# Attention stage of a fused kernel: half of q's copies by DMA, output transposes in groups, epsilon on VectorE, and a new order of instructions

## The chip, the core and the metric

The kernel runs on one core of one Trainium2 chip. A core has TensorE (PE, matmuls and transposes into PSUM), VectorE (DVE), ScalarE (ACT), GpSimd (POOL) and SyncE (SP), whose queue issues all the DMAs of this kernel. Each engine works through its own queue strictly in order. The metric is the device time of one execution in microseconds, as the median of several runs.

## What is computed

```python
def _attn_ref(q, k, v):            # 2 batches, 8 heads, 1152 positions, head size 64
    q_pool = q.reshape(B, H, S // 2, 2, D).mean(axis=3)
    scores = scale * np.matmul(q_pool, k.transpose(0, 1, 3, 2))
    attn = np.exp(scores - np.max(scores, axis=-1, keepdims=True))
    attn = attn / (np.sum(attn, axis=-1, keepdims=True) + 1e-09)
    return np.matmul(attn, v)
...
x = attn_out.transpose(0, 2, 1, 3).reshape(B * S, H * D)   # 1152 x 512
h = x @ w_in;  x = (h * np.clip(h + 3, 0, 6) / 6) @ w_out  # hidden size 2048
...
# then 8 experts (512 -> 1024 -> 512) weighted by a gate that is normalised 8 times over rows and columns
```

## The kernel before

The program has three stages: attention, the two-layer network, and the experts. The change is in the first, and in the order of the second.

**Attention.** Eight pairs n of (batch, two heads) are cut into nine units each, 72 units u in all. A unit is 128 rows of scores against 1152 keys. For each unit PE computes `scores` into one of two PSUM tiles `big` (line 359, six matmuls: q and k are split into a high and a low part that together keep float32 precision), DVE takes the row extreme (`rowmax`, L369), ACT the exponential (`expo`, L378), which also adds up the row sums. Then the 128x1152 block is split into two float16 parts: `high` on ACT (L283, hl<-p), `low` mostly on POOL (L291, hl<-p,hl), and a DMA transpose turns both (`across`, L391, pt<-hl). There are four `hl` and four `pt` tiles. Some units ("T" in the table `HIGHS`) are transposed by PE instead (`flip`, L397, with `flip_high` on ACT and `flip_low` on DVE, L408). PE then multiplies by v (`pv`, L420 and L421), into one of two PSUM banks `sm`.

**The output of attention.** For each chunk c of a pair (five to a pair, the last is 64 rows) DVE adds the three parts of the product (`gather`, L442) and divides by the row sums (`norm`, L451). PE transposes the chunk (`turn`, L457) into the same `sm` bank, ACT copies its high part (`x_hi`, L467), DVE makes the low part (`x_lo`, L471), and only then is the bank free. The row sums pass through `total` on ACT (L429, adds the epsilon) and `inverse` on DVE (L432) twice to a pair.

**Preparation of the next pair.** While a pair runs, the next pair's q, k and v are loaded (L303, L298, L308). q's two positions are added (`q_sum`, L324); `q_hi` (L285 on ACT, L287 on DVE) writes q's high part for each head into two halves of the partitions, four copies to a pair; `q_lo` (L293), `k_hi` (L283), `k_lo` (L291, kt<-raw,kt), `v_r1` and `v_r2` (L291, v<-v) make the rest. The tables `PREP`, `HIGHS` and `LOWS` name the engine of each step (S is ACT, V DVE, G POOL).

**What sets the order.** Every step is an entry in a plan (`Plan.add`) with an engine, an estimated cost and its dependencies. `Plan.run` gives each a rank, the longest way to the end by those costs, and draws the steps in time order; of the steps that can start, the one of the highest rank is put next into its engine's queue. A load is planned with `LOAD`, a DMA transpose with `TURN` (lead, transfer, tail). The plan only orders: on the chip each instruction waits for semaphores.

Of the kernel before, what the change touches and what calls it, by code (L numbers as in the profile page):

```python
# [9 lines left out]
F32 = mybir.dt.float32  # L10
# [11 lines left out]
SQ = S // 2  # L22
# [3 lines left out]
TB = 384  # L26
# [5 lines left out]
NP = 3  # L32
SLOTS = {"kt": (4, 1), "v": (2, 3), "p": (NP, 1), "hl": (4, 1), "pt": (4, 1), "pf": (2, 1)}
WARM = 9
LAG, PACE, PATIENCE = 0.2, 3.2, 0.0
PV_LAG, EARLY = 4, 3
HIGHS = [
    "STSTSSSVS", "SSSSSTSSS", "SSSSSTSSS", "SVSSSSTSS", "SSSSSTSSS", "SSSSSTSSS",
    "SSSSSTSSS", "STSSSTSVS",
]  # L40
LOWS = [
    "G.G.GGGGG", "GGGGG.VGG", "GGGGG.VGG", "GGGGGV.GG", "GGGGG.VGG", "GGGGG.VGG",
    "GGGGG.VGG", "G.GGG.GVG",
]
# [14 lines left out]
class Plan:  # L59
# [58 lines left out]
    def run(self):  # L118
# [69 lines left out]
def fused_kernel(ctx, tc, qd, kd, vd, w_in, w_out, w_gate, w1, w2, out):  # L188
# [72 lines left out]
    def attention(plan, xh, xl, xs, qv, qv_used, raw_keys, extra):  # L261
# [193 lines left out]
        def turn(n, c):  # L455
            w = width(c)
            nc.tensor.transpose(  # L457
                o_t[n, c][:, 384:384 + w], x_t[n][0:w, c].rearrange("p h d -> p (h d)"), ident[0:w, 0:w]
            )

        def x_out(n, c):
# [20 lines left out]
        def load_pair(n):  # L482
            kr, qr = raw_keys(0), raw_keys(1)
            if n == 0:
                h0, h1 = rows_of
                add("SP", 0.6, load_q, n, h0, w=[(qr, 0)], dma=(0.8, 0.85, 2.5))
                add("SP", 0.6, load_k, n, h0, slice(0, TB), w=[(kr, (0, 0))], dma=(0.8, 0.3, 2.5))
                add("SP", 0.6, load_k, n, h0, slice(TB, S), w=[(kr, (0, 1)), (kr, (0, 2))], dma=(0.8, 0.6, 2.5))
                add("SP", 0.6, load_q, n, h1, w=[(qr, 1)], dma=(0.8, 0.85, 2.5))
                add("SP", 0.6, load_k, n, h1, w=[(kr, (1, i)) for i in range(3)], dma=(0.8, 0.85, 2.5))  # L490
# [11 lines left out]
        def prep(n, kr, qr):  # L502
# [5 lines left out]
            for j in (0, 1):  # L508
# [4 lines left out]
                for i in thirds:  # L513
# [4 lines left out]
                for i in (0, 1):  # L518
# [10 lines left out]
        def front(u):  # L529
            n, c, j = units[u]  # L530
            i = u % 9
            if i == 0:
                S_[n] = plan.tile("sums", 3)
            js = (0, 1) if j is None else (j,)
            ps, nb, e = plan.tile("big", 2), plan.tile("nb", 4), new_slot("p")
            q = q_key[n % 2]
            add("PE", 1.04 * len(js), scores, u, pace=("unit", PACE),
                r=[(q, ("h", jj, a)) for jj in js for a in (0, 1)] + [(q, ("l", jj)) for jj in js]
                + [K[n][jj] for jj in js] + [qv_used], w=[ps])
            add("V", 1.43, rowmax, u, r=[ps], w=[nb, e])  # L540
            add("S", 1.41, expo, u, r=[ps, nb], w=[e, (S_[n], i)])
            return e
# [792 lines left out]
```

## Time and profile before

| what | value |
|---|---|
| median of 3 runs | 1293.03 us (1292.16 to 1296.89) |
| the profiled execution, its own time | 1296.86 us |
| its span, first to last instruction | 1295.1 us |
| PE busy | 1215.5 us (94%) |
| DVE busy | 941.1 us (73%) |
| ACT busy | 499.2 us (39%) |
| POOL busy | 194.3 us (15%) |

The shares are means over three stages that differ. POOL works only in the first 310 us, which is attention. A stretch in which PE is busy throughout can be shortened only by less PE work; one in which PE has gaps can be shortened by whatever fills them. The granted clock says at which share of its full rate TensorE ran.

### The profile page before, as it was taken

The page shows a single profiled execution, that of the slowest core. Times are in us where ns is not written, and L with a number is a line of the kernel's source. Part 1 is how long each engine was busy: PE and PEld are TensorE (multiplying, and loading weights), DVE is VectorE, ACT ScalarE, POOL GpSimd, SP SyncE. Part 2 cuts the span into 40 slices and gives each one's busy share as a digit, 9 for nine tenths or more (in the row PEclk, how much of TensorE's full clock was granted, in tenths as well). Part 3 has the DMA queues.
Part 4 walks back from the last instruction along what each step waited for, and adds up shares of the span by engine and source line. Part 5 has one row for each costly group of instructions (what it writes and reads, how often), then busy time and mean ns, then how long its engine had stood idle before and what let it go on. Part 6 is the DMA issues. An engine that isn't in the chain of part 4 may idle for free.

```text
span 1295.1 us, 18865 instructions
## 1 busy us (share of the span) xinstructions
PE 1215.5 (94%) x7718; PEld 1117.1 (86%) x7718; DVE 941.1 (73%) x1529; ACT 499.2 (39%) x745; POOL 194.3 (15%) x88
## 2 busy tenths in 40 slices
PE   6878878868999999989999999999999999999998
PEld 4767777757999999988899899899889989989987
DVE  7879887768999992897685576577568558657643
ACT  6867867754432441422232233124124223223310
POOL 5856676642000000000000000000000000000000
PEclk7889988889999999899999999999999999999999
DMA  5878969878323230101111011111111102101001
GB/s 146 176 159 179 210 131 189 174 167 136 105 95 110 93 110 17 49 17 34 66 66 49 18 64 50 45 37 49 49 33 66 33 33 66 50 21 62 1 1 73
DMA packets 161589, 104.64 MB, mean 81 GB/s; under 512 B 146848, under 2 KB 146912, under 8 KB 159584
## 3 DMA queue, kind: packets, MB, share of 16 engines
q1 hardware_dynamic: 161504, 103.45, 31.8%
q8 instruction: 60, 0.98, 0.3%
q14 instruction: 25, 0.20, 0.1%
HBM read 64.50 MB, written 2.36 MB: 52 GB/s over the span
## 4 chain that ended last, share of the span: by engine, by line
PE 80%; DVE 11%; issue 4%; DMA 3%; ACT 2%; POOL 1%; SPq 0%; DVEq 0%; POOLq 0%; ACTq 0%
PE sm L1164 30%; PE prod L1081 26%; PE big L816 8%; PE big L613 8%; PE sm L420 3%; DVE p L369 3%; PE big L359 2%; PE sm L421 2%; DMA pt<-hl 2%; DMA v<-vd 1%; DVE v L291 1%; ACT p L378 1%; PE sm L1196 1%; ACT hl L283 1%; DVE sm L442 1%
## 5 line engine op out<-in xcount | busy, mean ns | idle before, releaser
L1164 PE MATMUL sm<-w2h,slot 128*128 128x512 f32 x1152 | 355.0, 389 | 0.0
L1164 PEld LDWEIGHTS sm<-w2h,slot 128*128 128x128 f32 x1152 | 216.3, 188 | 44.6
L1164 PE MATMUL sm<-w2l,slot 128*128 128x512 f32 x576 | 224.2, 389 | 0.0
L1171 DVE SCALAR_TENSOR_TENSOR slot<-sm,gate,slot 128x512 f32<-128x512 f32 x120 | 89.9, 749 | 175.1 <-PE sm L1164 175.1
L1081 PE MATMUL prod<-xh,w_all 128*128 128x288 f32 x1024 | 194.7, 299 | 0.8 <-DVE slot L1100 0.6
L1081 PE MATMUL prod<-slot,w_all 128*128 128x288 f32 x1152 | 161.8, 293 | 0.0
L1081 PEld LDWEIGHTS prod<-xh,w_all 128*128 128x128 f32 x1024 | 158.8, 192 | 2.3 <-PE sm L1243 1.2
L1051 ACT CAST w2h<-raw 128x512 fp32r<-128x512 f32 x64 | 39.8, 623 | 303.3 <-PE sm L1164 296.9
L1081 PEld LDWEIGHTS prod<-slot,w_all 128*128 128x128 f32 x1152 | 155.1, 188 | 0.1
L291 POOL TENSOR_TENSOR hl<-p,hl 128x1152 f16<-128x1152 f32 x55 | 137.0, 2497 | 94.5 <-ACT hl L283 83.2
L359 PE MATMUL big<-kt,ql 128*128 128x384 f32 x240 | 97.9, 408 | 34.8 <-ACT p L378 26.6
L1164 PEld LDWEIGHTS sm<-w2l,slot 128*128 128x128 f32 x576 | 108.2, 188 | 21.9
L1100 DVE TENSOR_TENSOR slot<-slot,prod 128x576 f32<-128x576 f32 x160 | 119.6, 749 | 9.2 <-PE prod L1081 6.5
L420 PE MATMUL sm<-v,pt 128*128 128x192 bf16 (+1 forms) x630 | 101.0, 255 | 14.0 <-DVE pf L408 6.7
L1081 PE MATMUL prod<-xl,w_all 128*128 128x288 f32 x512 | 111.2, 299 | 0.0
L369 DVE TENSOR_SCALAR_CACHE_REDUCE p<-big 128x1152 bf16<-128x1152 f32 x72 | 96.8, 1350 | 15.8 <-PE big L359 11.5
L378 ACT ACTIVATE p<-big,nb 128x1152 f32<-128x1152 f32 x72 | 87.9, 1221 | 34.9 <-DVE p L369 34.7
L613 PE MATMUL big<-xh,w_all 128*128 128x384 f32 x384 | 100.3, 338 | 1.1 <-DVE slot L603 0.5
L421 PE MATMUL sm<-v,pt 128*128 128x128 bf16 (+1 forms) x630 | 98.8, 224 | 0.0
L359 PEld LDWEIGHTS big<-kt,ql 128*128 128x128 f32 x240 | 51.7, 215 | 45.2 <-ACT p L378 34.0
L359 PE MATMUL big<-kt,qh 128*128 128x384 f32 x240 | 89.8, 374 | 0.0
L1081 PEld LDWEIGHTS prod<-xl,w_all 128*128 128x128 f32 x512 | 83.9, 191 | 0.0
(124 smaller groups left out, 1860.4 us busy)
## 6 DMA issues: line engine op xcount, KB each, us to landing
raw<-w SPq DMA_DIRECT2D x64, 512.0 KB, 3.7
raw<-w_out SPq DMA_DIRECT2D x8, 1024.0 KB, 4.7
raw<-w_in SPq DMA_DIRECT2D x7, 1024.0 KB, 4.9
v<-vd SPq DMA_DIRECT2D x8, 576.0 KB, 4.7
raw<-qd SPq DMA_DIRECT2D x7, 576.0 KB, 4.6
raw<-kd SPq DMA_DIRECT2D x7, 576.0 KB, 4.7
out<-slot SPq DMA_DIRECT2D x8, 256.0 KB, 2.0
raw<-w_in SPq DMA_DIRECT2D x2, 512.0 KB, 5.3
```

The lines of the kernel that those rows point to most:

```text
L291: engines[eng].tensor_tensor(out, a, b, op=ALU.subtract)
L359: nc.tensor.matmul(ps[:, s, :TB], lhs, rhs[:, s * TB:(s + 1) * TB], start=m == 0, stop=m == len(mms) - 1,)
L369: nc.vector.tensor_scalar(waste, ps[:, :, :TB], PSHIFT * math.log(2.0), None, op0=ALU.add, op1=ALU.min, accum_out=nb)
L378: nc.scalar.activation(e_t[u], ps_t.pop(u)[:, :, :TB], AF.Exp, bias=nb_t.pop(u), scale=-1.0, accum_out=sums[n][:, i:i + 1])
L420: nc.tensor.matmul(ps, tt[:, k, q], vs, start=k == 0, stop=False)
L421: nc.tensor.matmul(ps[:, 0:2 * D], tt[:, NKC + k, q], vs[:, 0:2], start=False, stop=k == NKC - 1)
L613: nc.tensor.matmul(ps[t], lhs[:, ks], rhs[:, k, t * TB:(t + 1) * TB], start=k == 0 and m == 0, stop=k == KD - 1 and m == 2,)
L816: nc.tensor.matmul(downs[x, c][:, t, :TB], lhs[:, cs], rhs[:, t * TB:(t + 1) * TB], start=f == first and m == 0, stop=f == last and m == 2,)
L1081: nc.tensor.matmul(bank(q, p)[:, h], lhs, rhs[:, k, 288 * h:288 * h + 288], start=k == 0 and m == 0, stop=k == 1 and m == 2,)
L1100: nc.vector.tensor_tensor(base()[to], base()[u], bank(q, p), op=op)
L1164: nc.tensor.matmul(ps, lhs[:, ts], rhs, start=f == 0 and m == 0, stop=f == 3 and m == 2)
L1171: nc.vector.scalar_tensor_tensor(a, ps, gt, a, op0=ALU.mult, op1=ALU.add)
```

## The change

Five things change, all in attention. Two of the four copies of q's high part (from the second pair on) are no longer made by ACT or DVE but copied across partitions by a DMA on SP's queue (`q_dup`, "D" in `PREP`). The `turn` of four chunks goes into one `sm` bank of its own, so a pair has two turns, two `x_hi` and two `x_lo` in place of five of each (the last pair has three). `total` is gone from ACT: `inverse` adds the epsilon on DVE ahead of the reciprocal. The tables of engines are new: `v_r1` goes from POOL to DVE for seven pairs, one `k_lo` of each of these pairs from POOL to DVE, `q_sum` for five pairs from DVE to POOL; 12 units in place of 10 are transposed by PE. And the plan has a longer tail for loads, other costs for `scores` and `pv`, and a table `BIAS` that is added to the ranks by the name of a step.

```diff
-LAG, PACE, PATIENCE = 0.2, 3.2, 0.0
+LAG, PACE, PATIENCE = 0.2, 3.4, 0.0
+LOAD, TURN = (0.8, 1.7, 5.5), (0.8, 3.2, 0.8)
...
-    "STSTSSSVS", "SSSSSTSSS", "SSSSSTSSS", "SVSSSSTSS", "SSSSSTSSS", "SSSSSTSSS",
+    "STSTSVSSS", "TSSSSTSSS", "STSSSSSSS", "STSSSTSSS", "STSSSTSSS", "STSSSSSSS",
...
-    "SSVVVSSSSVVGG", "SSGGVSVSSVVGV", "SSGGVVSSSVVGV", "SSGGVSVSSVVGV", "SSVGVSSSSVVGV", "SSGGVVSVSVVGV",
+    "SSVVVSSVSVVGG", "VSGVGVDDVVVVV", "SSGVGSDDSVVVV", "VSGVVSDDSVVVV", "SSVVGSDDSVVVV", "SSGVGSDDVVVVV",
...
+BIAS = {
+    "rowmax": -1.2, "pv": 10.0, "q_sum": 5.8, "inverse": -9.4, "turn": 7.5,
...
+TURNS = [((0, 1, 2, 3), (4,)), ((0, 1), (2, 3), (4,))]
...
+        for o in ops:
+            rank[o["i"]] += BIAS.get(o["fn"].__name__, 0.0)
...
+        def q_dup(n, j, i):
+            q = qh[n % 2]
+            nc.sync.dma_start(out=f32(q[rows_of[i], j, cols_of[j]]), in_=f32(q[rows_of[j], j, cols_of[j]]))
...
-        def total(n, cols):
-            nc.scalar.activation(sums[n][:, cols], sums[n][:, cols], AF.Identity, bias=eps, scale=1.0)
-
         def inverse(n, cols):
+            nc.vector.tensor_scalar_add(sums[n][:, cols], sums[n][:, cols], EPS * 2.0 ** PSHIFT)
             nc.vector.reciprocal(sums[n][:, cols], sums[n][:, cols])
...
+        def turn(n, cs):
+            t = r_t[n, cs[0]] = small()
+            for i, c in enumerate(cs):
+                w = width(c)
+                nc.tensor.transpose(t[:, 128 * i:128 * i + w], x_t[n][0:w, c].rearrange("p h d -> p (h d)"), ident[0:w, 0:w])
...
+                    if e[f"q{j}{i}"] == "D":
+                        add("SP", 0.6, q_dup, n, j, i, r=[(q, ("h", j, j)), qv_used], w=[(q, ("h", j, i))], dma=(0.8, 0.5, LOAD[2] - 0.5))
+                        continue
...
-            add("PE", 1.04 * len(js), scores, u, pace=("unit", PACE),
+            add("PE", 1.12 * len(js), scores, u, pace=("unit", PACE),
...
+            for cs in TURNS[n == np_ - 1]:
+                if c == cs[-1]:
+                    out = plan.tile("sm", 2)
+                    parts = [(p, 5 * b + i) for i in cs]
+                    add("PE", 0.12 * len(cs), turn, n, cs, r=[(x, i) for i in cs] + [qv_used], w=[out])
+                    add("S", 0.13 + 0.13 * len(cs), x_hi, n, cs, r=[out], w=[(xs, ("h",) + i) for i in parts])
```

What this does to the queues is seen at three places. SP's queue before, from the load of the second pair's k on (`v<-vd` is the load of v, `raw<-kd` and `raw<-qd` of k and q, `pt<-hl` a transpose):

```order
L298 DMA raw<-kd 128x1152
L391 DMA_TRANSPOSE pt<-hl 128x18x128 x4
L298 DMA raw<-kd 128x1152
L303 DMA raw<-qd 128x1152
L391 DMA_TRANSPOSE pt<-hl 128x18x128 x8
L308 DMA v<-vd 128x1152
L298 DMA raw<-kd 128x1152
L303 DMA raw<-qd 128x1152
L391 DMA_TRANSPOSE pt<-hl 128x18x128 x7
```

SP's queue with the change, from the first transpose on (L410 is the transpose, L346 the copy `q_dup`, L323 the load of v, L313 of k, L318 of q):

```order
L410 DMA_TRANSPOSE pt<-hl 128x18x128 x2
L346 DMA qh_95<-qh_95 64x576 x2
L313 DMA raw<-kd 128x1152
L410 DMA_TRANSPOSE pt<-hl 128x18x128 x3
L318 DMA raw<-qd 128x1152
L410 DMA_TRANSPOSE pt<-hl 128x18x128 x2
L313 DMA raw<-kd 128x1152
L410 DMA_TRANSPOSE pt<-hl 128x18x128
L346 DMA qh_94<-qh_94 64x576
L410 DMA_TRANSPOSE pt<-hl 128x18x128
L346 DMA qh_94<-qh_94 64x576
L410 DMA_TRANSPOSE pt<-hl 128x18x128
```

The load of the fourth pair's k (the third `raw<-kd` before, the second here) goes from behind twelve transposes to behind seven; the load of the third pair's v, the next row of the queue, goes from behind twelve to behind ten, and the copies of q stand between transposes.

DVE's queue before, from the row extreme of unit 18 to that of unit 20 (L442 is `gather`, L451 `norm`, `v<-v` here is `v_r2`):

```order
L369 TENSOR_SCALAR p,nb<-big 128x1152
L293 SCALAR_TENSOR_TENSOR ql_98<-raw,qh_96 64x576
L408 TENSOR_TENSOR pf<-sm,pf 128x384
L432 RECIPROCAL sums<-sums 128x4
L442 TENSOR_REDUCE sm<-sm 128x128
L451 TENSOR_TENSOR x<-sm,sums 128x128
L369 TENSOR_SCALAR p,nb<-big 128x1152
L432 RECIPROCAL sums<-sums 128x5
L434 COPY sums<-sums 64x1
L291 TENSOR_TENSOR v<-v 128x1152
L369 TENSOR_SCALAR p,nb<-big 128x1152
L471 TENSOR_TENSOR xl<-sm,xh 128x128
```

DVE's queue with the change, from the row extreme of unit 18 to that of unit 20 (L388 is `rowmax`, L448 adds the epsilon, `v<-v` here is `v_r1`, `kt<-raw,kt` a `k_lo`):

```order
L388 TENSOR_SCALAR p,nb<-big 128x1152
L459 TENSOR_REDUCE sm<-sm 128x128
L468 TENSOR_TENSOR x<-sm,sums 128x128
L448 TENSOR_SCALAR sums<-sums 128x5
L449 RECIPROCAL sums<-sums 128x5
L451 COPY sums<-sums 64x1
L306 TENSOR_TENSOR v<-v 128x1152
L388 TENSOR_SCALAR p,nb<-big 128x1152
L459 TENSOR_REDUCE sm<-sm 128x128
L468 TENSOR_TENSOR x<-sm,sums 128x128
L339 TENSOR_TENSOR raw<-raw 128x576
L388 TENSOR_SCALAR p,nb<-big 128x1152
```

The epsilon is now a DVE row ahead of the reciprocal, no `xl<-sm,xh` stands here any more, and the `v<-v` in front of a row extreme is one that reads the load itself and not POOL's result.

ACT's queue before, over units 18 to 21 (`ACTIVATE p,sums` is `expo`):

```order
L378 ACTIVATE p,sums<-big,nb 128x1152
L283 CAST hl<-p 128x1152
L429 ACTIVATE sums<-sums,eps 128x5
L283 CAST kt<-raw 64x1152
L378 ACTIVATE p,sums<-big,nb 128x1152
L283 CAST kt<-raw 64x1152
L467 CAST xh<-sm 128x128
L283 CAST hl<-p 128x1152
L378 ACTIVATE p,sums<-big,nb 128x1152
L285 ACTIVATE qh_97<-raw 64x576
L283 CAST hl<-p 128x1152
L378 ACTIVATE p,sums<-big,nb 128x1152
```

ACT's queue with the change, over units 18 to 23 (L397 is `expo`, L298 a `high` or `k_hi`, L424 `flip_high`):

```order
L397 ACTIVATE p,sums<-big,nb 128x1152
L298 CAST hl<-p 128x1152
L298 CAST kt<-raw 64x1152
L397 ACTIVATE p,sums<-big,nb 128x1152
L300 ACTIVATE qh_95<-raw 64x576 x2
L397 ACTIVATE p,sums<-big,nb 128x1152
L424 CAST pf<-sm 128x384 x2
L298 CAST hl<-p 128x1152
L424 CAST pf<-sm 128x384
L397 ACTIVATE p,sums<-big,nb 128x1152
L298 CAST hl<-p 128x1152
L397 ACTIVATE p,sums<-big,nb 128x1152
```

Between two exponentials ACT now mostly holds one `high`; the epsilon is gone and `xh<-sm` is met twice to a pair.

## Rows read from the trace of the kernel before

**Rows 1.** Stretches: start:end, length, busy PE, PEld, DVE, ACT, POOL, clock, DMA, GB/s.

```profile
0.00:16.00 16.00, 8.14 (x20) 5.58 (x21) 11.58 (x16) 6.67 (x11) 6.83 (x13) 0.79 0.63 185
16.00:301.00 285.00, 226.30 (x1846) 202.49 (x1846) 225.76 (x345) 205.24 (x312) 184.77 (x74) 0.89 0.83 168
301.00:331.00 30.00, 24.77 (x244) 22.70 (x245) 27.79 (x57) 11.81 (x23) 2.70 (x1) 1.00 0.76 153
331.00:1295.00 964.00, 956.34 (x5612) 886.33 (x5609) 675.97 (x1114) 275.49 (x399) 0.00 (x0) 0.99 0.15 51
```

**Rows 2.** Waits in 16 to 301 us: engine, line, waited for, us, times, longest.

```profile
PE big L359 <- ACT p L378: 26.6, 18, 5.0
...
PE sm L457 <- DVE x L451: 9.0, 7, 2.3
POOL v L291 <- DMA v<-vd: 8.1, 1, 8.1
PE sm L420 <- DVE xl L471: 8.0, 5, 2.0
...
DVE sums L432 <- ACT sums L429: 7.2, 3, 2.7
...
ACT kt L283 <- DMA raw<-kd: 3.4, 2, 2.7
PE sm L397 <- DVE xl L471: 3.2, 2, 2.8
```

**Rows 3.** Timeline 79 to 92 us, SP, POOL, ACT, DVE: start, length, instruction, idle before.

```profile
80.09 0.57 SPq L308 DMA_DIRECT2D v<-vd  x1
...
84.78 2.11 POOL L291 TENSOR_TENSOR v<-v 128x1152 f32<-128x1152 f32 x1 [8.13 <-DMA v<-vd]
...
86.11 1.15 ACT L283 CAST kt<-raw 64x1152 fp32r<-64x1152 f32 x1 [2.74 <-DMA raw<-kd]
...
79.78 1.36 DVE L369 TENSOR_SCALAR_CACHE_REDUCE p<-big 128x1152 bf16<-128x1152 f32 x1 [0.30 <-PE big L359]
...
86.92 3.67 DVE L291 TENSOR_TENSOR v<-v 128x1152 bf16<-128x1152 f32 x1 [3.15 <-POOL v L291]
90.48 1.35 DVE L369 TENSOR_SCALAR_CACHE_REDUCE p<-big 128x1152 bf16<-128x1152 f32 x1
```

**Rows 4.** Groups by form, 16 to 301 us: count, busy us, mean ns, idle before.

```profile
L397 PE MATMUL sm<-ident,p 128*128 128x128 f32 x81 | 12.8, 288 | 6.2 <-DVE xl L471 3.2 <-DVE pf L408 2.7
L285 ACT ACTIVATE qh<-raw 64x576 fp32r<-64x576 f32 x23 | 15.7, 681 | 4.6 <-DVE raw L324 4.3
L291 DVE TENSOR_TENSOR v<-v 128x1152 bf16<-128x1152 f32 x7 | 17.5, 2506 | 3.2 <-POOL v L291 3.1
L291 DVE TENSOR_TENSOR hl<-p,hl 128x1152 f16<-128x1152 f32 x6 | 10.3, 1722 | 1.2 <-ACT hl L283 0.7 <-DMA raw<-qd 0.5
L291 DVE TENSOR_TENSOR kt<-raw,kt 64x1152 fp32r<-64x1152 f32 x1 | 1.4, 1351 | 0.0
L324 DVE TENSOR_TENSOR raw<-raw 128x576 f32<-128x576 f32 x7 | 13.8, 1974 | 0.1
L408 DVE TENSOR_TENSOR pf<-sm,pf 128x384 f16<-128x384 f32 x27 | 14.4, 549 | 0.6 <-ACT pf L405 0.5
L432 DVE RECIPROCAL sums<-sums 128x5 f32<-128x5 f32 x7 | 1.3, 186 | 7.2 <-ACT sums L429 7.2
L471 DVE TENSOR_TENSOR xl<-sm,xh 128x128 fp32r<-128x128 f32 x27 | 7.5, 285 | 9.6 <-ACT xh L467 9.5
L471 DVE TENSOR_TENSOR xl<-sm,xh 128x64 fp32r<-128x64 f32 x6 | 1.3, 218 | 1.4 <-ACT xh L467 1.4
```

**Rows 5.** Line 291 up to 320 us: shortest/median/longest ns.

```profile
L291 POOL TENSOR_TENSOR hl<-p,hl x55: 2361/2383/4257, 19.6 to 310.0; 128x1152 f16<-128x1152 f32 x55
...
L291 DVE TENSOR_TENSOR v<-v x7: 1476/2098/3673, 31.5 to 268.4; 128x1152 bf16<-128x1152 f32 x7
```

**Rows 6.** DMA issues up to 330 us: count, KB each, median us to landing.

```profile
raw<-qd SPq DMA_DIRECT2D x2, 288.0 KB, 4.4
```

More of the change, by code (lines that the diff above doesn't have):

```diff
@@ L53 @@
 }
+BIAS = {
+    "rowmax": -1.2, "pv": 10.0, "q_sum": 5.8, "inverse": -9.4, "turn": 7.5,
+    "gate_l": -7.6, "q_dup": 12.1, "v_r1": -7.6, "dec_low": 3.9, "dec_rest": 7.0,
+    "total": 11.6, "norm": 8.7, "load_k": -0.8, "load_q": 8.4, "flip": -8.8,
+    "k_lo": 9.9, "dec_scale": 3.8, "dec_m": -1.9, "x_lo": -0.2, "low": 8.9,
+    "x_hi": 8.4, "gather": -4.5, "up_one": -1.6, "dec_e": -0.8, "load_v": -3.4,
+    "expo": -8.5, "across": 7.3, "gate_m": -0.4, "dec_high": -0.7, "flip_high": 12.8,
+    "dec_sign": 13.6, "k_hi": 12.8, "gate_s": -6.1, "gate_h": 8.4, "v_r2": 2.2,
+    "q_lo": -2.5, "dec_join": 14.2, "q_hi": 8.9, "scores": 7.4, "flip_low": 1.0,
+    "high": 3.5,
+}
+TURNS = [((0, 1, 2, 3), (4,)), ((0, 1), (2, 3), (4,))]
 W2_TILES = 6
@@ L211, in fused_kernel @@
     nc.vector.memset(half, 0.5)
-    eps = per.tile([128, 1], F32, name="eps")
-    nc.vector.memset(eps, EPS * 2.0 ** PSHIFT)
     rebias = per.tile([128, 1], F32, name="rebias")
@@ L343, in attention @@
             units.append((n, 4, None))
-        ps_t, nb_t, sums, e_t, h_t, p_t, o_t, x_t, f_t = {}, {}, {}, {}, {}, {}, {}, {}, {}
+        ps_t, nb_t, sums, e_t, h_t, p_t, o_t, x_t, f_t, r_t = {}, {}, {}, {}, {}, {}, {}, {}, {}, {}
         def scores(u):
@@ L453, in norm, with x_out, x_hi, x_lo @@
             )
[L455 to L461, printed above, removed]
+        def turn(n, cs):
[3 more added lines that the diff above has]
+                nc.tensor.transpose(t[:, 128 * i:128 * i + w], x_t[n][0:w, c].rearrange("p h d -> p (h d)"), ident[0:w, 0:w])
+        def x_out(n, cs):
             b, p = pairs[n]
-            return o_t[n, c][:, 384:384 + width(c)], (p, slice(b * SQ + 128 * c, b * SQ + 128 * c + width(c)))
-        def x_hi(n, c):
-            ps, (p, o) = x_out(n, c)
+            w = 64 if cs[0] == 4 else 128 * len(cs)
+            return r_t[n, cs[0]][:, 0:w], (p, slice(b * SQ + 128 * cs[0], b * SQ + 128 * cs[0] + w))
+        def x_hi(n, cs):
+            ps, (p, o) = x_out(n, cs)
             nc.scalar.copy(xh[:, p, o], ps)
-        def x_lo(n, c):
-            ps, (p, o) = x_out(n, c)
+        def x_lo(n, cs):
+            ps, (p, o) = x_out(n, cs)
             nc.vector.tensor_tensor(xl[:, p, o], ps, f32(xh[:, p, o]), op=ALU.subtract)
@@ L485, in load_pair @@
                 h0, h1 = rows_of
[L486 to L490, printed above, removed]
+                add("SP", 0.6, load_q, n, h0, w=[(qr, 0)], dma=(0.8, 0.85, LOAD[2]))
+                add("SP", 0.6, load_k, n, h0, slice(0, TB), w=[(kr, (0, 0))], dma=(0.8, 0.3, LOAD[2]))
+                add("SP", 0.6, load_k, n, h0, slice(TB, S), w=[(kr, (0, 1)), (kr, (0, 2))], dma=(0.8, 0.6, LOAD[2]))
+                add("SP", 0.6, load_q, n, h1, w=[(qr, 1)], dma=(0.8, 0.85, LOAD[2]))
+                add("SP", 0.6, load_k, n, h1, w=[(kr, (1, i)) for i in range(3)], dma=(0.8, 0.85, LOAD[2]))
             else:
@@ L517, in prep @@
                             w=[(t, ("h", p)) for p in ps], share=share)
-                for i in (0, 1):
+                for i in (j, 1 - j):
+                    if e[f"q{j}{i}"] == "D":
+                        add("SP", 0.6, q_dup, n, j, i, r=[(q, ("h", j, j)), qv_used], w=[(q, ("h", j, i))], dma=(0.8, 0.5, LOAD[2] - 0.5))
+                        continue
                     prep_op("q_hi", e[f"q{j}{i}"], q_hi, n, j, e[f"q{j}{i}"], i, r=[(qr, j), qv_used], w=[(q, ("h", j, i))])
@@ L566, in rear @@
             for u in us:
-                add("PE", 2.6 / len(us), pv, u, r=[P[u], V[n]], w=[(sm, "a")])
+                add("PE", 2.8 / len(us), pv, u, r=[P[u], V[n]], w=[(sm, "a")])
             if c in (0, 2):
@@ L570, in rear @@
                 parts = [(s, i) for i in range(cols.start, cols.stop)]
-                add("S", 0.2, total, n, cols, w=parts)
-                add("V", 0.17, inverse, n, cols, w=parts + ([(s, 9)] if c == 2 else []))
+                add("V", 0.25, inverse, n, cols, w=parts + ([(s, 9)] if c == 2 else []))
             add("V", 0.565, gather, n, c, r=[(sm, "a")], w=[(sm, "b")])
             add("V", 0.29, norm, n, c, r=[(sm, "b"), qv_used] + [(s, i) for i in ((2 * c, 2 * c + 1) if c < 4 else (8, 9))], w=[(x, c)])
-            add("PE", 0.15, turn, n, c, r=[(x, c), qv_used], w=[(sm, "b")])
             b, p = pairs[n]
-            part = (p, 5 * b + c)
-            add("S", 0.26, x_hi, n, c, r=[(sm, "b")], w=[(xs, ("h",) + part)])
-            add("V", 0.285, x_lo, n, c, r=[(sm, "b"), (xs, ("h",) + part)], w=[(xs, ("l",) + part)])
+            for cs in TURNS[n == np_ - 1]:
[4 more added lines that the diff above has]
+                    add("S", 0.13 + 0.13 * len(cs), x_hi, n, cs, r=[out], w=[(xs, ("h",) + i) for i in parts])
+                    add("V", 0.13 + 0.14 * len(cs), x_lo, n, cs, r=[out] + [(xs, ("h",) + i) for i in parts],
+                        w=[(xs, ("l",) + i) for i in parts])
         pending = []
```

8 lines of the change are left out of this document (4 added, 4 removed).

## The prediction

> **What bounds the kernel now.** I read the stretches first [rows 1]. From 331 us to the end PE is busy for 956 of 964 us at a clock of 0.99, so nothing that the change moves there can win more than 8 us, and I count that part as unchanged. Attention's steady part, 16 to 301 us, is another matter: DVE, the busiest, has 225.8 us of work in 285, PE 226.3, ACT 205.2, POOL 184.8. No engine is full. The time is made by engines that wait for each other in order, and PE's 58.7 us without work, at a clock of 0.89, are all that can be won there. The 72 units take 4.0 us each.
>
> The second view is who waits for whom in that stretch [rows 2]. PE waits 26.6 us for an exponential that frees its score tile. PE also waits where the output leaves: 9.0 us for `norm` before a `turn`, and 8.0 and 3.2 us for `x_lo` to free an `sm` bank. DVE waits 7.2 us, in three waits, for the epsilon on ACT. POOL stands 8.1 us in one wait for a load of v.
>
> The third view is the timeline of the widest gap between two row extremes, 79.78 to 90.48 us [rows 3]. The load of v is issued at 80.09 behind the transposes, POOL's `v_r1` can start at 84.78 only, DVE's `v_r2` stands in its queue behind that until 86.92 and takes 3.67 us, and the next row extreme comes at 90.48. On ACT a k load that is 2.74 us late holds the next exponential.
>
> **The change part by part.** The epsilon: `total` leaves ACT, so the three waits of DVE go: **-7.2 us** [rows 2]. What takes their place is an add in DVE's own queue, counted below.
>
> The turns: 40 round trips PE, ACT, DVE, PE become 17 (two for each of seven pairs, three for the last), and a bank of `pv` is free after `norm` and not after `x_lo`. Of the 20.2 us that PE waits in these three rows [rows 2] I take off the share of trips that go, 23 of 40: **-11.6 us**. The bounds are 0, if the same stall moves to the new bank, of which there are still two for all uses, and 20.2.
>
> The late landings: loads of k stand earlier in SP's queue and `v_r1` is planned for a later landing. The gap of 10.7 us [rows 3] against 4.0 for a unit gives **-6.7 us**; 0 if another wait ends last there, 10.1 with ACT's 3.4 us for k [rows 2] on top.
>
> ACT's work: 15 of the 27 `q_hi` go from ACT, at 0.681 us [rows 4] 10.2 us of its 205, 5%. I take 5% off PE's 26.6 us of waiting for the exponential: **-1.3 us**. At best half of that wait goes, 13.3.
>
> DVE's work, what speaks against: seven `v_r1` come from POOL, at the 2.506 us of `v_r2`, which has the same shape in: 17.5. Seven `k_lo` come too; DVE ran one of that form, in 1.351, and the same operation on 128 partitions (`low`) in 1.722 on the mean; I take 1.722, since the one had a lucky place: 12.1. Four `low` go (-6.9) and five `q_sum` at 1.974 (-9.9). Six more `flip_low` at 0.549 are 3.3, sixteen adds of the epsilon at most a reciprocal's 0.186 each, 3.0. `x_lo` costs 0.285 for 128 columns and 0.218 for 64, so about 0.69 for 512 and 0.42 for 256: -3.5 over all pairs. One `q_hi` and two `k_hi` more, under `k_lo`'s 1.351 each, 3.0 together. The sum is 18.6 [rows 4]. Part of it falls into DVE's idle time; I put on the path DVE's busy share, 225.8 of 285 or 0.79: **+14.7 us**. The bounds are 0 (all of it into the 59 us that DVE idles) and 24.1 (`k_lo` at 2.506 too, all on the path).
>
> Why such an operation takes 1.476 us at its shortest and 2.506 on the mean: POOL runs 2.383 us pieces beside it [rows 4, 5]. The Trainium skill says on "SBUF — State Buffer", section "SBUF: two separate sides", that VectorE operations with two SBUF inputs and GpSimd's share one port pair as an exclusive lock that is held for the whole instruction. The trace agrees in direction, with 1.0 us lost on the mean and not a whole piece of POOL. By the rule at its worst the sum would end slower; that is the first rival.
>
> What I count at nothing: the 14 copies of q by DMA. The nearest load, 288 KB, lands in 4.4 us [rows 6]; the third pair's copies stand behind the eighth and ninth transposes, and its own first transpose is the fifteenth, so five to six units of 4.0 us lie between. Without that cover each of seven pairs would start up to 4.4 us late, 31 us. Each issue takes SP some 0.57 us [rows 3], 8 in all, spread over 285. Six more PE transposes of three blocks for two units more are 18 at 0.288 us, 5.2 at most [rows 4], hidden in PE's 58.7 us without work; if PE were full they would cost that. The last pair sends nine blocks by DMA transpose and not seven, and DVE is busy there for 27.8 of 30 us [rows 1]; PE's 5.2 us without work there are what can be won, and I take the like for a loss: 0, plus or minus 5. A better clock would come with shorter gaps: 0.10 of PE's 226 us, up to 23, but only where PE is what ends last; 0.
>
> **The sum.** -7.2 - 11.6 - 6.7 - 1.3 + 14.7 = -12.1 us, against the profiled execution's own 1296.9: 1284.8. That execution lies 3.8 above the median of 1293.0, so the forecast is 1281. All gains at their best and DVE's work hidden would be -51 (7.2 + 20.2 + 10.1 + 13.3), 1242; only the epsilon's gain and 24.1 on the path +17, 1310.
>
> **The rivals.** First, slower: DVE becomes the bound because what came from POOL waits behind POOL. If each of the 14 operations waits for a whole piece, `v_r1` takes 1.476 + 2.383 and `k_lo` 1.351 + 2.383 us: 53.1 in place of 29.6, DVE's addition 42.1 and not 18.6. At 0.79 of that on the path against the 26.8 of gains it gives +6.5, 1299; with all of it +15.3, 1308; I call it 1304. For it: the longest of them took 3.673 [rows 5], and they stand right in front of a row extreme. Against it: POOL loses 14 operations, so there is less to wait behind. It decides from an addition of 34 us on (26.8 / 0.79). This is the lock as the Trainium skill states it on "SBUF — State Buffer", taken at its worst.
>
> Second, no change: the stalls move and do not go. DVE's work of 225.8 + 18.6 = 244.4 us needs an idle share under 12% to make the stretch shorter by more than 7 us (244.4 / 0.88 = 278), and above 16% the stretch is longer (291). Today it is 21%. Between these two it gives 1287 to 1299, about 1293. For it: ACT and DVE still serve one score tile of two in turn. Against it: the waits of the first three terms have a cause that is taken away.
>
> Third, a larger gain: with shorter round trips PE gets the whole 20.2 us and half the 26.6 back, the added DVE work falls half into idle time (9.3): -7.2 - 20.2 - 6.7 - 13.3 + 9.3 = -38, 1255; halfway to the forecast, 1268, is what I expect of it. For it: gaps feed on each other in queues, and PE runs at 0.89. Against it: at 1268 DVE would have to be busy for 94% of the stretch (244.4 of 260).
>
> The copies of q may land late after all: up to +31 less 12, 1312. Their place in the queue speaks against it.
>
> **How the numbers follow.** The forecast's case, 1272 to 1287, 0.45; the larger gain 0.17; no change 0.20; DVE behind POOL 0.15; late copies 0.03. A measurement of this kernel tells about 0.5% (6.5 us) from no change; the three runs lie 0.4% apart. Faster by more than that is 0.45 + 0.17 = 0.62, within it 0.20, slower 0.18. The range leaves out the outer half of the two slower cases and the tail of the larger gain: 1259 to 1303; the forecast's own is 1272 to 1287.
>
> **What would show it.** In the profile after: no wait of DVE's reciprocal for ACT; PE's waits for `norm` and `x_lo` together under 10 us; no wait of several us on a load of v or k; 17 `x_lo`; DVE's busy time up to 331 us some 19 us higher, or more if `v_r1` and `k_lo` on DVE average above 2.5 us, which is the first rival; no wait of PE on a copy of q. The start of the stretch in which PE is never idle, 331 us now, should come about 12 us earlier. The forecast is wrong if DVE's waiting for PE and for ACT's high copies grows by what the terms take away.

## The result, and the profile after

| | before | with the change |
|---|---|---|
| median | 1293.9 us (4 runs, 1292.2 to 1296.9) | 1277.6 us (4 runs, 1275.0 to 1279.8) |
| ratio | | 0.986, 95% interval 0.984 to 0.989 |

The change makes the kernel 1.4% faster, 16.3 us, where 12 were forecast. The stretches of the changed kernel, cut where those of [rows 1] were cut (columns as there):

```profile
0.00:16.00 16.00, 7.22 (x16) 4.95 (x17) 11.99 (x16) 5.98 (x10) 6.68 (x13) 1.00 0.55 152
16.00:285.00 269.00, 223.92 (x1871) 201.17 (x1871) 244.28 (x358) 192.95 (x271) 168.34 (x66) 0.93 0.93 181
285.00:315.00 30.00, 26.49 (x246) 24.59 (x244) 24.05 (x47) 9.13 (x15) 4.71 (x2) 0.96 0.71 144
315.00:1277.00 962.00, 954.24 (x5608) 882.73 (x5606) 676.80 (x1116) 275.92 (x399) 0.00 (x0) 1.00 0.15 52
```

The last stretch, in which PE is never idle, is as long as before (962 against 964 us) and begins 16 us earlier. So the whole gain lies in attention's steady part, 269 us against 285. PE's work in it is the same (223.9 against 226.3 us, at a granted clock of 0.93 against 0.89); DVE has 18.5 us more work and idles for 9% instead of 21%.

The waits of that part (engine, line, waited for, us, times, longest), which answer to [rows 2]:

```profile
ACT p L397 <- DVE p L388: 56.6, 34, 5.7
...
PE big L378 <- ACT p L397: 21.9, 17, 3.1
...
PE sm L416 <- DVE x L468: 4.8, 4, 2.0
...
PE sm L476 <- DVE x L468: 2.9, 2, 1.5
ACT hl L298 <- DMA pt<-hl: 2.7, 3, 1.7
...
PE sm L439 <- DVE xl L489: 1.3, 1, 1.3
...
PE sm L416 <- DVE xl L489: 0.2, 1, 0.2
```

L476 is `turn`, L439 `pv`, L416 `flip`. The waits that the forecast named are smaller or gone: no reciprocal waits for ACT, none on a load of v or k stands here any more, and the waits for `norm` and `x_lo`, 20.2 us before, are 2.9, 1.3 and 0.2, with 4.8 new where a `flip` waits for `norm` to free a bank. One wait that it did not name fell too, that of ACT's `high` for a DMA transpose to free an `hl` tile. It is 2.7 us here. And one wait grew, that of ACT's exponential for DVE's row extreme, as fits a stretch in which DVE has become the busiest engine. The rows of before:

```profile
ACT p L378 <- DVE p L369: 31.6, 29, 6.1
...
ACT hl L283 <- DMA pt<-hl: 20.8, 8, 6.3
```

DVE's groups by form (columns as [rows 4]), again from 16 to 285 us of the changed kernel:

```profile
L306 DVE TENSOR_TENSOR kt<-raw,kt 64x1152 fp32r<-64x1152 f32 x8 | 18.4, 2300 | 0.2
L306 DVE TENSOR_TENSOR v<-v 128x1152 bf16<-128x1152 f32 x7 | 12.8, 1828 | 0.0
L306 DVE TENSOR_TENSOR v<-v 128x1152 f32<-128x1152 f32 x7 | 11.2, 1594 | 0.1
...
L448 DVE TENSOR_SCALAR sums<-sums 128x5 f32<-128x5 f32 x7 | 6.7, 957 | 0.0
L448 DVE TENSOR_SCALAR sums<-sums 128x4 f32<-128x4 f32 x8 | 5.9, 740 | 0.0
L489 DVE TENSOR_TENSOR xl<-sm,xh 128x512 fp32r<-128x512 f32 x7 | 4.8, 680 | 0.0
```

The two rows of L448 are the surprise: an add over four or five columns takes 0.74 and 0.96 us on the mean, 12.6 us together. Over the whole of attention, up to 331 us before and up to 315 with the change, DVE's busy time rises by 15.2 us, 265.1 to 280.3, where 18.6 were forecast. Of q's new copies little is to be seen: a copy of 144 KB lands 2.8 us after its issue, and nothing waits for one.

The gap of 10.7 us in [rows 3], which the prediction calls the widest, is the second widest of before: the starts of the row extremes show nine gaps of over 6 us there, and the widest, 11.9, begins at 274.9 us. With the change there are seven, the widest 9.0.

One sentence on the change ahead of the prediction is wrong, and the prediction drew on it: the plan has no longer tail for loads. The new table `LOAD` with 5.5 us stands at the head of the file, but a line `LOAD = (0.8, 1.7, 2.5)` further down, which the diff does not touch and so does not show, hides it in the function that makes the plan. The late landings are not counted at all.

### The profile page after: what moved, and what is told of

It is laid out like the page before. It is cut to its first block, busy times and chain, and to the rows that moved or that the text cites. A ratio compares the mean times of both kernels' runs of the same rounds, so it can differ in the third digit from the quotient of the medians.

```text
span 1277.9 us, 18850 instructions
## 1 busy us (share of the span) xinstructions
PE 1211.9 (95%) x7736; PEld 1113.4 (87%) x7736; DVE 957.1 (75%) x1534; ACT 484.0 (38%) x694; POOL 179.7 (14%) x81
## 4 chain that ended last, share of the span: by engine, by line
PE 75%; DVE 16%; issue 4%; DMA 2%; ACT 1%; POOL 1%; SPq 0%; POOLq 0%; DVEq 0%; ACTq 0%
PE sm L1188 31%; PE prod L1105 26%; PE big L840 7%; PE big L637 4%; DVE p L388 4%; PE big L378 3%; PE sm L439 2%; DMA pt<-hl 2%; DVE kt L306 1%; PE sm L440 1%; DVE sm L459 1%; DVE sums L448 1%; DVE pf L427 1%; DVE v L306 1%; DVE slot L630 1%
## 5 line engine op out<-in xcount | busy, mean ns | idle before, releaser
L1188 PE MATMUL sm<-w2h,slot 128*128 128x512 f32 x1152 | 355.0, 389 | 0.0
L306 POOL TENSOR_TENSOR hl<-p,hl 128x1152 f16<-128x1152 f32 x57 | 146.9, 2585 | 102.5 <-ACT hl L298 76.0
L1188 PEld LDWEIGHTS sm<-w2l,slot 128*128 128x128 f32 x576 | 108.1, 188 | 21.9
L378 PE MATMUL big<-kt,ql 128*128 128x384 f32 x240 | 96.0, 400 | 27.2 <-ACT p L397 21.9
L397 ACT ACTIVATE p<-big,nb 128x1152 f32<-128x1152 f32 x72 | 87.9, 1221 | 60.0 <-DVE p L388 59.4
L388 DVE TENSOR_SCALAR_CACHE_REDUCE p<-big 128x1152 bf16<-128x1152 f32 x72 | 96.9, 1350 | 16.8 <-PE big L378 14.8
L439 PE MATMUL sm<-v,pt 128*128 128x192 bf16 (+1 forms) x612 | 98.5, 257 | 8.2 <-DVE pf L427 4.7
```

Of the source, the lines that this page charges most:

```text
L306: engines[eng].tensor_tensor(out, a, b, op=ALU.subtract)
L378: nc.tensor.matmul(ps[:, s, :TB], lhs, rhs[:, s * TB:(s + 1) * TB], start=m == 0, stop=m == len(mms) - 1,)
L388: nc.vector.tensor_scalar(waste, ps[:, :, :TB], PSHIFT * math.log(2.0), None, op0=ALU.add, op1=ALU.min, accum_out=nb)
L397: nc.scalar.activation(e_t[u], ps_t.pop(u)[:, :, :TB], AF.Exp, bias=nb_t.pop(u), scale=-1.0, accum_out=sums[n][:, i:i + 1])
L439: nc.tensor.matmul(ps, tt[:, k, q], vs, start=k == 0, stop=False)
L1188: nc.tensor.matmul(ps, lhs[:, ts], rhs, start=f == 0 and m == 0, stop=f == 3 and m == 2)
```

## The experiments

Every kernel is an edit of the changed one; ratios are to the kernel before, measured again beside each (medians 1294.2 to 1295.9 us), with their 95% intervals. The last column is the start of the last row extreme, from the `rowmax` line of each profile; the last instruction of the profiled execution comes 989 to 996 us after it, but for one kernel (e2, 1006), so it says where the time went. A profile is of one execution; the changed kernel's took 1279.7 us, 2.1 above its median.

| run | edit | median us | ratio | last row extreme, us |
|---|---|---|---|---|
| (before) | | 1293.9 | 1 | 306.1 |
| (changed) | | 1277.6 | 0.986 (0.984 to 0.989) | 287.5 |
| e6_no_bias | `BIAS` empty | 1301.2 | 1.004 (1.002 to 1.005) | 309.3 |
| e11_bias_nine_tenths | `BIAS` times 0.9 | 1286.0 | 0.993 (0.991 to 0.995) | 292.6 |
| e10_late_counted | the local `LOAD` taken out | 1279.8 | 0.990 (0.987 to 0.994) | 286.1 |
| e4_turns_single | one turn for each chunk | 1314.8 | 1.015 (1.013 to 1.018) | 313.5 |
| e12_no_bias_turns_single | both e6 and e4 | 1315.8 | 1.016 (1.013 to 1.019) | 317.6 |
| e1_eps_on_act | the add on ACT | 1277.5 | 0.987 (0.985 to 0.989) | 285.4 |
| e3_no_eps | no add | 1263.1 | 0.975 (0.974 to 0.977) | 269.4 |
| e2_eps_accumulating | add in its accumulating form, new tile | 1280.3 | 0.988 (0.987 to 0.990) | 273.1 |
| e5_eps_accumulating_in_place | the same without a new tile | 1268.4 | 0.979 (0.976 to 0.981) | 273.3 |
| e7_v_r1_on_pool | `v_r1` on POOL | 1272.3 | 0.983 (0.980 to 0.986) | 278.6 |
| e9_best | e5 and e7 | 1271.5 | 0.982 (0.980 to 0.984) | 273.4 |
| e8_q_copies_on_act | q's copies on ACT | 1278.1 | 0.987 (0.984 to 0.989) | 281.9 |

The theory to be tested was that of the prediction: the time comes from stalls that the parts of the change remove, less DVE's added work. The main rival was that the gain comes from the order, whatever the parts do.

**The order.** In e6 all parts stay and the table is empty:

```diff
-BIAS = {
-    "rowmax": -1.2, "pv": 10.0, "q_sum": 5.8, "inverse": -9.4, "turn": 7.5,
...
+BIAS = {}
```

> The changed kernel with the table of biases empty, so the plan orders by its costs alone; all parts of the change are in. If the parts make the gain, as the prediction's terms have it, 1278 to 1284. If the drawn order makes it, this run loses most of the gain: 1290 or more.

Waits of e6 from 16 to 307 us (L368 is `scores`, L288 `high`, L438 the add):

```profile
PE big L368 <- ACT p L387: 28.8, 17, 6.4
ACT hl L288 <- DMA pt<-hl: 22.1, 10, 4.1
...
DVE sums L438 <- ACT p L387: 6.8, 5, 3.9
```

Without the table the parts are 0.4% slower than the kernel before, and the waits for the exponential and for the `hl` tiles are back at 28.8 and 22.1 us; the adds now wait 6.8 us for an exponential's row sums. All of the gain, 23.6 us against e6, is there only with the table. Whether it states rules or fits one drawing was asked with e11, which multiplies each value by 0.9:

```diff
-            rank[o["i"]] += BIAS.get(o["fn"].__name__, 0.0)
+            rank[o["i"]] += 0.9 * BIAS.get(o["fn"].__name__, 0.0)
```

> The changed kernel with every value of BIAS times 0.9, a control for what a new drawing of the order costs by itself. If the table states a rule about which step goes first, nine tenths of it say nearly the same: 1274 to 1283. If the table fits one drawn order, it gives much of the gain back: 1285 to 1300, between the changed kernel and the one without the table (1301), with PE waiting for the exponential for over 25 us.

Waits of e11 from 16 to 290 us:

```profile
PE big L378 <- ACT p L397: 14.3, 12, 4.4
PE sm L416 <- DVE pf L427: 10.0, 6, 3.3
PE sm L416 <- DVE x L468: 9.8, 5, 2.9
PE sm L476 <- DVE x L468: 7.5, 6, 1.9
...
PE sm L439 <- DMA qh<-qh: 7.0, 1, 7.0
```

1286.0: a tenth off its values loses half of the 16 us that the changed kernel gains, as expected of a table that fits one drawing. The rival said that PE would wait over 25 us for the exponential; it waits 14.3, so that part of it is wrong. Other waits took over, one of them on a late copy of q by DMA, 7.0 us. From this control on, a difference of up to some 8 us between two kernels that draw different orders says little about the edit between them.

The third drawing is e10, in which the late landings are counted after all:

```diff
-    LOAD = (0.8, 1.7, 2.5)
+    pass
```

> The changed kernel without the local line LOAD = (0.8, 1.7, 2.5), which hides the table of the same name at the head of the file, so that the plan now does count 5.5 us behind a load; the order is drawn anew, nothing else. Theory of the prediction's third term (counting late landings takes the gaps at k and v away): the waits for loads in the changed kernel's steady stretch are already small (POOL 7.0 us once, ACT 0.5), so at most 2 to 7 us, 1271 to 1276. Rival (the table BIAS fits the one order that it was drawn with, and any other order loses what it gave): between 1285 and 1301, with more gaps over 6 us than the 7 of the changed kernel and no wait on a load behind them.

Waits of e10 from 16 to 284 us:

```profile
PE big L378 <- ACT p L397: 24.5, 15, 3.8
ACT hl L298 <- DMA pt<-hl: 16.0, 13, 4.9
```

1279.8, between both expectations and not told apart from the changed kernel: the intervals overlap. Counting the landings wins nothing here, and it does not lose as much as the rival said either: it has seven gaps of over 6 us, as many as the changed kernel. So the table is not tied to one drawing alone; this other drawing keeps most of the gain, while e11's loses half of it. ACT's wait for `hl` tiles is at 16.0 us again, and the time hardly moved, so that wait alone does not explain the table's gain. Which of the waits does stays open.

**The turns.** e4 goes back to one turn for each chunk, in its own order:

```diff
-TURNS = [((0, 1, 2, 3), (4,)), ((0, 1), (2, 3), (4,))]
+TURNS = [((0,), (1,), (2,), (3,), (4,))] * 2
```

> The changed kernel with one chunk to a turn again, each in an sm bank of its own (five turns, five x_hi and five x_lo to a pair); the plan draws a new order for it with the same biases. By the prediction's term the round trips cost 11.6 us, less what DVE already has them at: 1277.6 + 11.6 + 2.8 (3.5 us of x_lo at 0.79) = 1292. The rival, that the new order made the gain and the grouping none, gives 1278 to 1281.

Waits of e4 from 16 to 315 us:

```profile
ACT hl L298 <- DMA pt<-hl: 18.7, 8, 5.4
PE sm L476 <- DVE x L468: 18.0, 10, 4.3
DVE sm L459 <- PE sm L440: 17.9, 14, 3.3
```

The stall at the turn is back, 18.0 us where 2.9 were. But 37 us is far above the forecast's 20.2 at most, and the order was drawn anew with a table made for other steps. e12 takes the table out of the comparison with both edits:

> The changed kernel with BIAS empty and with a turn for each chunk, to be read against the run with BIAS empty alone (1301.2). The prediction's second term (23 of 40 round trips, 11.6 us, up to 20.2): 1313, up to 1321, with PE waiting for norm and x_lo for about 20 us. Rival (what single turns cost with the table, 37 us, was mostly the new order): within 5 us of 1301.

Waits of e12 from 16 to 315 us (L466 is `turn`, L479 `x_lo`):

```profile
ACT hl L288 <- DMA pt<-hl: 35.3, 15, 5.7
...
PE sm L466 <- DVE x L458: 13.8, 8, 2.8
...
PE sm L406 <- DVE xl L479: 7.4, 5, 2.7
```

1315.8 against e6's 1301.2: grouping the turns is worth 14.6 us without the table, inside the forecast's bounds and near its 11.6, and PE's waits for `norm` and `x_lo` are 21.2 us again. This pair too differs in its drawing, so the 14.6 carry the control's uncertainty. The rest of e4's 37 us is the table, which does not fit single turns: with it they take as long (1314.8) as without it.

**The epsilon.** e1 puts only the add back on ACT, at its place in the order:

```diff
-            nc.vector.tensor_scalar_add(sums[n][:, cols], sums[n][:, cols], EPS * 2.0 ** PSHIFT)
+            nc.scalar.activation(sums[n][:, cols], sums[n][:, cols], AF.Identity, bias=eps, scale=1.0)
```

> The changed kernel with the epsilon added on ACT again, at the place in the order where DVE adds it; all else stands where it stood. By the prediction's term DVE waits for ACT again (7.2 us before the change) and sheds the adds, which it put at 3.0 us: about 1277.6 + 5 = 1283. The rival is that the adds on DVE cost what the wait cost: the changed kernel's trace shows 12.8 us for 16 of them (149 ns the shortest, 2396 ns the longest), so shedding them gives back more than the wait takes: 1270 to 1278.

The wait of the reciprocal (L451) for ACT in e1:

```profile
DVE sums L451 <- ACT sums L450: 9.9, 12, 1.6
```

The wait is back, and the time is the same: 1277.5. So this edit is worth nothing as made, since DVE pays as much for the adds as it waited. Why an add of five columns can cost so much is seen in the timeline of the changed kernel, at three of the sixteen (start, length, instruction; the rows of POOL and of L448 alone):

```profile
49.49 2.37 POOL L306 TENSOR_TENSOR hl<-p,hl 128x1152 f16<-128x1152 f32 x1 [1.25 <-ACT hl L298]
50.97 0.92 DVE L448 TENSOR_SCALAR sums<-sums 128x5 f32<-128x5 f32 x1
...
163.81 2.38 POOL L306 TENSOR_TENSOR hl<-p,hl 128x1152 f16<-128x1152 f32 x1 [2.06 <-ACT hl L298]
166.96 0.16 DVE L448 TENSOR_SCALAR sums<-sums 128x4 f32<-128x4 f32 x1
...
261.54 4.85 POOL L306 TENSOR_TENSOR hl<-p,hl 128x1152 f16<-128x1152 f32 x2 [4.43 <-DVE x L468]
264.03 2.39 DVE L448 TENSOR_SCALAR sums<-sums 128x5 f32<-128x5 f32 x1
```

The first add starts in the middle of a POOL piece and ends with it, at 51.89 against 51.86. The second starts when POOL is between two pieces and takes 0.16. The third ends with POOL's second piece, 266.42 against 266.39. Seven of the sixteen are held up so, each until 0.03 us after a piece has ended; nine take 0.15 to 0.20 us. The add waits for the whole rest of POOL's piece.

The Trainium skill says on "SBUF — State Buffer", section "Who interferes with whom", that VectorE's `tensor_scalar`, but not the form that also writes out its accumulator, can take the port pair that it shares with GpSimd, and that whichever of the two comes first then holds it for its whole instruction while the other is blocked. The trace agrees with the blocking, in these seven adds. e3, e2 and e5 test the rest of it. e3 leaves the epsilon out of the row sums:

```diff
-            nc.vector.tensor_scalar_add(sums[n][:, cols], sums[n][:, cols], EPS * 2.0 ** PSHIFT)
```

> The changed kernel with the addition of the epsilon left out (the row sums go into the reciprocal as they are), all else in place. The same 12.8 us of DVE go entirely: 1266 if DVE's busy share sets the time, 1278 if the wait only moves to the next instruction of DVE that needs what POOL holds (then v_r1, v_r2, k_lo and q_lo on DVE get longer by about as much).

1263.1, 14.5 us faster than the changed kernel, for 12.8 us of adds. e2 keeps the add and gives it an accumulator that nobody reads:

```diff
-            nc.vector.tensor_scalar_add(sums[n][:, cols], sums[n][:, cols], EPS * 2.0 ** PSHIFT)
+            junk = ap.tile([128, 1], F32, tag="junk", name="junk", bufs=2)
+            nc.vector.tensor_scalar(
+                sums[n][:, cols], sums[n][:, cols], EPS * 2.0 ** PSHIFT, None, op0=ALU.add, op1=ALU.min, accum_out=junk
+            )
```

> The changed kernel with the epsilon added on DVE in the form that also writes an accumulator (as the row extreme does), result the same. If the 12.8 us of the 16 adds are a wait for POOL that depends on the form of the instruction, they fall to about 0.17 us plus 0.08 us for the accumulator, 4 us in all, and with DVE busy for 91% of the stretch the time falls by some 8 us, to 1270. If any small operation at that place waits so, the adds stay at some 12 us and the time at 1278. If DVE's share is not what ends last, the adds get short and the time stays at 1278.

The last row extreme comes 14 us earlier than in the changed kernel, but the median is 1280.3. The gain is lost much later, in the experts. Their largest group of matmuls in the changed kernel, and then in e2:

```profile
L1188 PE MATMUL sm<-w2h,slot 128*128 128x512 f32 x1152 | 355.0, 389 | 0.0
```

```profile
L1191 PE MATMUL sm<-w2h,slot 128*128 128x512 f32 x1152 | 363.0, 397 | 0.0
```

The same 1152 matmuls take 397 ns each and not 389, at the same granted clock of 1.00. The only thing that e2 adds beside the adds' form is the tile `junk`, two buffers of 4 bytes a partition; e1, e3 and e4, run on the same chip without it, have 389. e5 writes the accumulator into a column of `sums` that is not in use then:

```diff
-                sums[n][:, cols], sums[n][:, cols], EPS * 2.0 ** PSHIFT, None, op0=ALU.add, op1=ALU.min, accum_out=junk
+                sums[n][:, cols], sums[n][:, cols], EPS * 2.0 ** PSHIFT, None, op0=ALU.add, op1=ALU.min,
+                accum_out=sums[n][:, 9:10]
```

> The epsilon on DVE in the accumulating form again, but the accumulator goes into the spare column of the row sums, so that no tile is allocated and no address moves. In the run with a tile of its own the adds fell to 0.15 us each and attention's last row extreme came at 273.2 us instead of 287.5, but the matmuls of 512 columns in the experts took 397 ns instead of 389, 1728 of them or 13.8 us, which gave the gain back. If the tile's address did that, this run has the short adds and 389 ns: 1263 to 1267. If the accumulating form costs something of its own, it stays at 1278.

The adds in e5 (shortest/median/longest ns, first and last start):

```profile
L448 DVE TENSOR_SCALAR_CACHE_REDUCE sums<-sums x16: 135/148/160, 36.6 to 285.4; 128x4 f32<-128x4 f32 x8, 128x5 f32<-128x5 f32 x8
L448 DVE DVE_READ_ACCUMULATOR sums<-sums x16: 72/82/85, 36.7 to 285.5; 128x1 f32 x16
```

None is held up any more: 160 ns at the longest, against 2396 in the plain form, which agrees with the exception that the Trainium skill makes for this form (same page and section). The median is 1268.4, 9.2 us under the changed kernel, the fastest here that computes the whole reference, and the matmuls are back at 390 ns.

The adds are not the only operation that is held up. `q_hi` on DVE is a plain `tensor_scalar` too, and its rows (as above) show it before the change, in the changed kernel and in e5:

```profile
L287 DVE TENSOR_SCALAR qh<-raw x5: 453/867/2841, 31.0 to 171.4; 64x576 fp32r<-64x576 f32 x5
```

```profile
L302 DVE TENSOR_SCALAR qh<-raw x6: 442/967/2794, 6.7 to 215.9; 64x576 fp32r<-64x576 f32 x6
```

```profile
L302 DVE TENSOR_SCALAR qh<-raw x6: 455/2408/2866, 6.8 to 205.1; 64x576 fp32r<-64x576 f32 x6
```

In the changed kernel and in e5 those of over 1 us end 0.31 to 0.32 us after the POOL piece that they meet. In e5 the six take 12.2 us together and not 8.2, so a part of what the adds gave back is lost there. Whether an accumulator helps `q_hi` too was not tried.

**`v_r1`.** e7 gives the seven back to POOL, at their place in the order:

```diff
         def v_r1(n, eng):
+            eng = "G"
             minus(eng, v_raw[n][:, 1], v_raw[n][:, 0], v_t[n][:, 0])
```

> The changed kernel with the seven v_r1 on POOL again, each where it stood in the order. By the prediction's term for DVE's work this is a gain: DVE sheds 11.2 us, at its busy share of 0.91 some 10 us, 1267. The rival is that POOL, with 7 x 2.1 = 15 us more in its queue ahead of the low parts, makes the transposes late: 1285 or more.

1272.3, some 5 us better, with intervals that just overlap (0.980 to 0.986 against 0.984 to 0.989). Moving `v_r1` to DVE did not pay, then, and may have cost a little. DVE sheds 11.2 us of `v_r1` here, but in all it is busy for 6.1 us less (957.1 to 951.0), since `q_lo` and `q_hi` take 7.6 us more. With e5's adds beside it, e9:

> The changed kernel with two edits together: the epsilon's add in its accumulating form, with an unused column of sums as the accumulator, and v_r1 on POOL again for all pairs. Theory (the adds' 12 us and v_r1's time on DVE are two separate costs on the same critical queue): 1268.4 with the first alone, 5 less for the second, about 1263; the add at about 150 ns; the last row extreme before 272 us. Rival (they are the same slack: with the add gone DVE has room for v_r1, and POOL's load of v becomes the wait): 1267 to 1272, POOL waiting 9 us or more for v.

1271.5, no gain over e5's 1268.4. The rival's median fits, but not its cause: POOL waits 9.8 us for loads of v in all, but 7.3 of it in the first 16 us, where the changed kernel has 7.0 of its own; the steady stretch has one such wait of 2.5. The two savings do not add up. Part of the reason stands in DVE's rows from 16 to 271 us (L308 is `q_lo`, `v<-v` is `v_r2`), first of e5, then of e9:

```profile
L308 DVE SCALAR_TENSOR_TENSOR ql<-raw,qh 64x576 fp32r<-64x576 f32 x14 | 18.4, 1316 | 0.2
...
L306 DVE TENSOR_TENSOR v<-v 128x1152 bf16<-128x1152 f32 x7 | 12.8, 1824 | 0.0
```

```profile
L308 DVE SCALAR_TENSOR_TENSOR ql<-raw,qh 64x576 fp32r<-64x576 f32 x14 | 23.8, 1702 | 0.2
...
L306 DVE TENSOR_TENSOR v<-v 128x1152 bf16<-128x1152 f32 x7 | 15.5, 2221 | 0.0
```

With `v_r1` POOL is busy for 182.2 and not 167.4 us of this stretch, and these two operations on DVE take 8.1 us more, nearly the 9.4 that `v_r1` took there in e5; that POOL's work is what lengthens them is likely, but was not tested by itself. Others, `q_hi` among them, get shorter, so DVE's work does fall, 234.1 to 226.5 us, but the stretch stays 255 us and DVE idles more. That agrees with the first half of the rival, that DVE has room once the adds are short; which wait ends last then was not found.

**The copies of q.** e8 makes them on ACT and not by DMA:

```diff
-            nc.sync.dma_start(out=f32(q[rows_of[i], j, cols_of[j]]), in_=f32(q[rows_of[j], j, cols_of[j]]))
+            nc.scalar.copy(q[rows_of[i], j, cols_of[j]], f32(q[rows_of[j], j, cols_of[j]]))
```

> The changed kernel with the 14 copies of q made by ACT, from the first copy and at the same place in the order, in place of the DMAs. ACT has 14 x 0.68 = 9.5 us more. The prediction counted 1.3 us for ACT's part: 1279. If ACT's place between two exponentials is worth more, each copy delays one exponential by 0.7 us: up to 1287. If the DMAs were late, 1278 or less.

1278.1, the same. ACT is busy for 193 of the changed kernel's 269 us, so it has room for the copies, and the DMAs win nothing.

## Why the prediction was right, point by point

The forecast of 1281 is 3.4 us from the median, and its place is right: the stretch that PE fills begins 16 us earlier (forecast 12). But that is in part luck: two terms of the sum are wrong in their cause, and the largest contribution is not in it.

- **Epsilon, -7.2.** The wait went, as said. The step that failed is "sixteen adds of the epsilon at most a reciprocal's 0.186 each, 3.0": they took 12.8, since they wait behind POOL's pieces. e1 puts the edit's worth at 0. The reciprocal was the nearest row by size, but it is never held up (177 to 192 ns in e5); the add is another form. A row of the add's own form stood in the trace of before: `q_hi` on DVE, 0.453 us at the shortest and 2.841 at the longest.
- **Turns, -11.6.** Right in mechanism and near in size. The named waits fell from 20.2 to 9.2 us, with the new wait of `flip` counted, 11.0 less; e12 against e6 gives 14.6.
- **Late landings, -6.7.** The waits on v and k are gone from the steady stretch, but the step "`v_r1` is planned for a later landing" is wrong: the plan's tail is as before. For v the place in the order did most of it: in e7, with `v_r1` on POOL again at its place, POOL's wait for a load in the steady stretch is 2.2 us, where 8.1 were. In e6, without the table, 6.4 us of waits on loads are back, half of them on k, none over 1.9. Counting the landings (e10) wins nothing. What this gap alone was worth was not measured.
- **ACT's work, -1.3.** PE's wait for the exponential fell by 4.7 us, 26.6 to 21.9. The copies of q, to which the term was tied, are worth nothing (e8); without the table the wait is 28.8 (e6).
- **DVE's work, +14.7.** The added work was forecast as 18.6 and measured as 15.2 us over attention (18.5 in the steady stretch, but the 30 us behind it hold 3.7 less). That it came so near is partly luck: `v_r1` took 1.594 us each and not 2.506, `k_lo` 2.300 and not 1.722, the adds four times their price, and `q_lo` and `v_r2`, which the forecast left as they were, 9.6 us less together. The 0.79 on the path has no single value. DVE's busy time in all falls by 14.4 us in e3, and 14.5 are won; by 11.4 in e5, for 9.2; by 6.1 in e7, for some 5; but by 14.5 in e9, for 6.1, and by 12.3 in e1, for none, since DVE waits for ACT there. (Before the change PE, at 226.3 us, was a little busier than DVE at 225.8; the sum does not depend on it.)
- **The order, no term.** The prediction gave the table no term. e6 shows it worth 23.6 us with these parts: more than the whole gain. Without it the kernel is 0.4% slower than before, some 5 us, where the sum of terms said -12; the 5 lie inside the 8 us that another drawing can make, the 17 us between the two do not. No run gives the kernel before a table of its own, so how much the order alone would win without the parts stays open.

Of the rivals, DVE behind POOL is real as a mechanism, in the adds above all, but the addition stayed under its 34 us: the seven `v_r1` and seven `k_lo` added 28.2 us, near the forecast's 29.6 and far from the rival's 53.1. The stalls did not just move: DVE's idle share is 9%, under the 12% from which that rival was excluded. The larger gain is in number what e5 reaches, 1268, with DVE busy for 234 of 255 us, 92%, but by short adds and not by the shorter round trips that this rival names. A late copy of q did not show in the changed kernel, but did once in e11.

## What to carry to other kernels

Price a small VectorE operation by the longest row of its own form beside GpSimd's pieces and not by another operation of its size, and where it is held up, try the form that writes an accumulator. A table of ranks may fit the steps, costs and values that it was made with (nine tenths of its values lost half the gain here): before an edit is judged in a kernel that has one, draw the order again with slightly other values, to know how much of the difference any new order makes. And follow a constant to the line that uses it, since a diff does not show a later line that hides it.

## What the runs showed of the hardware that was not expected

A VectorE `tensor_scalar` over 128x4 or 128x5 float32 values takes 149 ns alone and up to 2396 ns when it meets a GpSimd piece, whose end it then shares to within 0.03 us; with an accumulator output it takes 135 to 160 ns, beside the same pieces. A plain one over 64x576 (`q_hi`) took 456 ns alone and up to 2866 beside a piece.

With one more tile of two buffers of 4 bytes a partition, matmuls of 128x512 took 397 ns and not 389, 363.0 and not 355.0 us over 1152 of them, at a granted clock of 1.00 in both. That it comes from where later tiles lie in SBUF is likely, since nothing else changed for them, but it was only argued; e1 adds a tile of 4 bytes in another pool and does not show it in its time.
